# Order and timing of loads, 16-row broadcasts, a pool for unit 29 and a bank left out, in the last stage of an attention block with a gated MLP

## The chip, the cores and the metric

The kernel runs on one core of a Trainium2 chip. TensorE (PE) multiplies matrices into PSUM, VectorE (DVE), ScalarE (ACT) and GpSimd (POOL) work on tiles, and SyncE (SP) issues nearly all DMAs from one queue, in program order. The metric is the device time of one execution in microseconds (us). Before the change it is 1626.81 us, the median of three runs (1626.63 to 1628.37).

## The reference

```python
x = A_x                                   # (1, 2048, 512)
xn = layernorm(x)
s = attention(xn, A_wqkv) @ A_wo          # 32 heads of 16, softmax(q k^T / 4) v
h = relu(xn @ B_w1 + B_b1) ** 2           # 1792 wide
g = silu(h @ B_w2 + B_b2)
return x + s * g
```

Both branches read the normalised rows; the output joins them. All arithmetic is in float32: the kernel splits operands of projections into a high and a low part and multiplies them in three terms.

## The kernel before

Attention is cut into 32 units: a unit is four heads (a group, `qd = u // 4`) by 512 query columns (`qc = u % 4`). Units run one after the other. Each takes 16 slots, one for each block of 128 keys, so there are 512 slots, and slot `st` belongs to unit `st // 16`. In a slot PE computes scores for the exponentials (`exp_mm`, line 1260, exponential on ACT at line 1272), the scores again for row maxima of a unit further on (`max_mm`, line 320, maximum on DVE at line 327), the product of probabilities with v of two slots earlier (`pv_mm`, line 406, eight records a slot at the slot's end), and a share of the dense work that `dense()` hands out. PE, DVE, ACT, POOL and SP all keep the order in which the program was written.

The maxima of a unit end nine slots or so before it starts. `max_end` then puts the unit into `late` with a due time; when that comes, `shift` turns the maxima on DVE (lines 371 to 374), `keep` stores them to `sh_d` one slot later (line 380), and `back` reads them into the rows of `qe` (line 397, four small DMAs). Exponentials of a unit may start two slots after `back`. `later(n, fn)` runs `fn` at the start of the slot n slots on; everything due at one slot runs in the order in which it was put there, ahead of what the slot itself issues. A DMA whose wait isn't over holds all DMAs behind it on SP.

A unit's result leaves PSUM by `evac` (line 416) and is divided by its sums: these are stored to `r_d` (line 435), read back as a broadcast over 32 rows for each of four heads into the upper half of `hl` (line 440), and multiplied on POOL (line 446); POOL then splits the product (447, 448), and it is stored to `on_d` (455). Unit 29 goes another way: `unit_mid` copies it, and six slots later `unit_turn` transposes it on DVE (line 827) into the tiles `ttm0` and `ttm1`, so that sums can be divided there. Units 30 and 31 end in the same helper with other tiles.

Dense work: the MLP fills slots 4 to 451. Slots 452 and 453 have none. The output projection follows. `wo_part` (slots 454 to 485) computes 16 tiles of 128 rows by 512, k = 4c + tt, two slots a tile, with the first three quarters of the depth (three pieces `on_d[0..2]`, line 697, for column block c). `wo_load(c, ...)` brings the three pieces for a block: two into halves of a `ka` buffer, one into an `oc` buffer, 512 KB each; block 0's in two parts, at slot 452, and block c + 1 one piece a slot. `wo_ask(k)` asks for a tile's gate rows g (line 724) and its rows of x (`xr`, line 727, three buffers). When a tile is done, ACT copies it (line 774), POOL multiplies by g and adds xr (775, 776), and SP stores it to `sp_d` (778). `wo_last` (slots 486 to 510) adds the last quarter: PE, then a product on DVE that empties the bank (line 796), a sum (798), and the store of the output.

In `wo_part` four PSUM banks are shared by the projection tile and the row maxima. `bank()` takes the one that was taken longest ago, other than the current tile's. Tile 15 always takes `last_bank`.

Memory is handed out by pools on two stacks. `o3` holds the buffers `oc` and `xr` until slot 486; then `q6p` and `endp` open on the freed bytes.

These lines set the special slots:

```python
RUN = 454
PAIR = (484, 485)
MAXIMA = {465: 5, 481: 5, 484: 2, 485: 0}
TWO = (2, 3, 452, 453)
GAPS = (24,)
```

Of the kernel before, what the change touches and what calls it, by code (L numbers as in the profile page):

```python
# [9 lines left out]
F32 = mybir.dt.float32  # L10
F32R = mybir.dt.float32r
AF = mybir.ActivationFunctionType
ALU = mybir.AluOpType
# [4 lines left out]
P = 128  # L18
# [3 lines left out]
DH = 16  # L22
# [5 lines left out]
NU = NQ * 4  # L28
# [29 lines left out]
def kernel(  # L58
# [11 lines left out]
    nc = tc.nc  # L70
# [44 lines left out]
    with ExitStack() as ph:  # L115
# [81 lines left out]
        late = []  # L197
# [4 lines left out]
        def later(n, fn):  # L202
            if n:
                waiting.append((now[0] + n, fn))
            else:
                fn()
# [124 lines left out]
        def max_end(g):  # L331
            for u in [u for u, n in left.items() if n == 0]:
                del left[u]
                m4 = m4s[u % 2]
                nc.vector.tensor_reduce(m4[:, :16], mxs[u], axis=AX.X, op=ALU.max)
                mxs[u] = m4
                late.append((g + {0: 0, 3: 8, 29: 0, 30: 2, 31: 0}.get(u, 6), u))
            u, s = divmod(g, 16)
            if u >= NU:
                return  # L340
            qd, qc = divmod(u, 4)
            if qd == 0:
                if qc == 2 and s % 2 == 0 and s < 12:
                    load_k(1, s // 2)
                if qc == 3 and 9 <= s < 15:
                    load_k(1, s - 3)
            else:
                if qc == 2 and qd + 1 < NQ and s % 2 == 0:
                    load_k(qd + 1, s // 2)
                if qc == 3 and qd + 1 < NQ and s % 2 == 0 and s < 8:  # L350
                    load_k(qd + 1, 8 + s // 2)
            if u == 3 and s == 8:
                for j in range(2):
                    rows = slice(64 * j + 3 * DH, 64 * j + 4 * DH)
                    nc.sync.dma_start(
                        rot["ka"][3][rows, :].bitcast(F32), rot["ka"][2][rows, :].bitcast(F32)
                    )
            at = (12, 14) if u == 1 else (8, 9)
            if s in at:
                load_q_pair(u, "qe", at.index(s), qes.setdefault(u, []))  # L360
            at = (6, 10) if u == 1 else (7, 11)
            if s in at and u + 1 < NU:
                load_q_pair(u + 1, "qm", at.index(s), qms.setdefault(u + 1, []))
# [73 lines left out]
        def evac_back(u, ev):  # L437

            ev["hl"] = pools["n"].tile([P, 2, 512], F32R, name="hl")
            nc.sync.dma_start(  # L440
                ev["hl"][:, 1].bitcast(F32), r_d[u][:, None, :].to_broadcast([4, 32, 512])
            )

        def evac_norm(u, ev):
            ot, hl = ev["ot"], ev["hl"]
            nc.gpsimd.tensor_tensor(ot, ot, hl[:, 1].bitcast(F32), op=ALU.mult)  # L446
            nc.gpsimd.tensor_scalar(hl[:, 0], ot, 1.0, 0.0, op0=ALU.mult, op1=ALU.add)
            nc.gpsimd.tensor_tensor(hl[:, 1], ot, hl[:, 0].bitcast(F32), op=ALU.subtract)

# [184 lines left out]
        def right(stk, name, bufs):  # L634
            return stk.enter_context(tc.tile_pool(name=name, bufs=bufs, side="right"))
# [15 lines left out]
        def wo_pools():  # L651
            wos["f"] = right(wstk, "fp", 4)
            wos["oc1"] = right(wstk, "oc1p", 1)
            tp = tail["p"] = right(wstk, "tailp", 1)
            for tt in range(4):
                tail[3, tt] = tp.tile([P, D], F32, name=f"ts{tt}")
            left = ph.enter_context(tc.tile_pool(name="xpl", bufs=1))
            more = [left.tile([P, 512], F32, name=f"xl{i}") for i in range(3)]
            pool = right(wstk, "xpr", 1)
            more += [pool.tile([P, 512], F32, name=f"xr{i}") for i in range(NXR)]  # L660
            more += [vs["tiles"][0][:, 512 * i : 512 * i + 512] for i in range(2)]
            rot["pt"] = more + rot["pt"]
            wos["oc3"] = right(o3, "oc3p", 2)

        def wo_small():
# [53 lines left out]
        def wo_ask(k):  # L719

            c, tt = divmod(k % 16, 4)
            t0 = c * 512 + tt * P
            g = wos["f"].tile([P, D], F32, name="g", bufs=6)
            nc.sync.dma_start(g, g_d[t0 : t0 + P, :])
            if k < 16:
                t = wos["oc3"].tile([P, D], F32, name="xr", bufs=3)
                nc.sync.dma_start(t, xf[t0 : t0 + P, :])
            elif c < 3:
                t = wos["f"].tile([P, D], F32, name="s")
                nc.sync.dma_start(t, sp_d[t0 : t0 + P, :])  # L730
            else:
                t = tail[c, tt]
            wos[k] = g, t

        def bank():
            mine = wos["banks"]
            n = next(n for n, t in enumerate(mine) if t is not wos["tile"])
            mine.append(mine.pop(n))
            return mine[-1]

        def wo_part():
            wos["banks"] = [pm.tile([P, 512], F32, name="pm_t") for _ in range(3)]
            wos["banks"].append(pd.tile([P, 512], F32, name="pd_t"))
            last_bank = wos["banks"][2]
            wos["tile"] = None
            for c in range(4):
                for tt in range(4):
                    k = 4 * c + tt
                    if c < 3 and tt == (1 if c == 0 else 0):
                        wo_load(c + 1, [0, 1, 2])  # L750
                    if k < 14:
                        wo_ask(k + 2)
                    if k == 14:
                        wo_load(0, [3])
                        wo_ask(16)
                        wo_ask(17)
                    old = wos["tile"]
                    if k < 15:
                        ps = bank()
                        if old is not None:  # L760
                            wos["banks"].sort(key=lambda t: t is old)
                    else:
                        ps = last_bank
                        wos["banks"].sort(key=lambda t: t is last_bank)
                    wos["tile"] = ps
                    t0 = c * 512 + tt * P
                    g, xr = wos.pop(k)
                    if c == 3:
                        s = tail[c, tt]
                    else:  # L770
                        s = wos["f"].tile([P, D], F32, name="s")

                    def post():
                        nc.scalar.activation(s, ps, AF.Copy)
                        nc.gpsimd.tensor_tensor(s, s, g, op=ALU.mult)
                        nc.gpsimd.tensor_tensor(s, s, xr, op=ALU.add)
                        if c < 3:
                            later(2, lambda s=s, t0=t0: nc.sync.dma_start(sp_d[t0 : t0 + P, :], s))

                    yield from halves(wo_terms(ps, wos["t", c], tt, [0, 1, 2]), (9,), post, 1)  # L780
            wos["banks"] = None
# [29 lines left out]
        def load_q6(c):  # L811

            q = wos["q", c] = wos["q6"].tile([P, 2, 512], F32R, name=f"q6{c}")
            for h in range(2):
                nc.sync.dma_start(
                    q[64 * h : 64 * h + 64].bitcast(F32),
                    on_d[3][:, :64, c * 512 : (c + 1) * 512].rearrange("k p t -> p k t"),
                )
# [2 lines left out]

        def unit_turn(po, i, which=""):

            t = tail["e"].tile([P, 256], F32, name=f"tt{which}{i}")
            nc.vector.transpose(t, po[:, 256 * i : 256 * i + 256])
            sm = tail["e"].tile([P, 8], F32, name=f"tsm{which}{i}")
            return t.rearrange("p (b r) -> p b r", r=32), sm

        def unit_back(ot, rows, sm):
# [640 lines left out]
        def dense():  # L1472
            mp = ExitStack()
            yield from mlp_tasks(mp)
            mp.close()
            early.close()
            wo_pools()
            wo_load(0, [0, 1, 2])
            wo_ask(0)
            wo_ask(1)  # L1480
            for _ in range(2):
                yield [], None
            later(10, wo_small)
            yield from wo_part()
            for c in range(3):
                if c == 0:
                    o3.close()
                    wos["q6"] = right(wstk, "q6p", 1)
                    tail["e"] = right(wstk, "endp", 1)
                    later(10, lambda: load_q6(3))  # L1490
                yield from wo_last(c)

# [212 lines left out]
```

## Time and profile before

| | |
|---|---|
| median of three runs | 1626.81 us (1626.63 to 1628.37) |
| profiled execution | 1627.33 us |
| its span, first to last instruction | 1625.5 us |
| granted TensorE clock, mean | 0.999 |
| PE, DVE, ACT, POOL busy | 99%, 84%, 73%, 32% |
| DMA over the span | 209.45 MB, mean 129 GB/s |

How rows read: a timeline row has the start in us from the span's start, the duration, the engine, the line, the operation, what it writes and reads, and the count of merged instructions; in brackets stands idle time of the engine just before, and what ended it. SPq rows are DMA issues, not transfers. Matmuls overlap, so rows of PE overlap too. A windows row has, for a stretch, the busy time and count of PE, PE's weight loads, DVE, ACT and POOL, the granted clock, the mean busy share of the 16 DMA engines and the GB/s that they moved. A waits row has who waited for whom: us in total, times, the longest. A row of the groups has busy time, mean ns, and idle time before.

### The profile page before, as it was taken

Reading aid. Unit: us, or ns where it says so; the run is one execution under the profiler, and the core shown is the slowest. Engines: PE = TensorE matmul, PEld = TensorE weight load, DVE = VectorE, ACT = ScalarE, POOL = GpSimd, SP = SyncE. Lnnn points to the kernel's source line nnn. Section 1 sums busy time; section 2 is a strip of 40 time slices with the busy share of each in tenths; the row PEclk is TensorE's granted clock in tenths of the full one; section 3 lists DMA queues with packets and bytes.
Section 4 is the critical chain, followed back from the end, with each engine's and each line's share of the span. In section 5 each row is a group of like instructions: output and inputs, shape, how many; then the busy total and the mean of one; then the engine's idle time right before and its main releaser. Section 6 shows DMA issues by size and latency. Waiting matters only on the chain.

```text
span 1625.5 us, 36023 instructions
## 1 busy us (share of the span) xinstructions
PE 1609.1 (99%) x13660; PEld 936.6 (58%) x13660; DVE 1362.3 (84%) x2363; ACT 1189.8 (73%) x2350; POOL 521.9 (32%) x550
## 2 busy tenths in 40 slices
PE   8999999999999999999999999999999999999998
PEld 6899665556545654664466456645654565445543
DVE  6486888888888888888888888888888888887755
ACT  7212777777777777877777777777777777778876
POOL 6437667133113310321133112311331133214521
PEclk9999999999999999999999999999999999999999
DMA  8877556434333333434333334423442252237664
GB/s 301 232 237 233 173 163 157 127 95 130 79 104 97 101 93 85 128 87 110 83 114 96 87 87 126 116 66 84 131 122 62 73 157 72 61 109 225 186 197 168
DMA packets 164036, 209.45 MB, mean 129 GB/s; under 512 B 59000, under 2 KB 78968, under 8 KB 162296
## 3 DMA queue, kind: packets, MB, share of 16 engines
q1 hardware_dynamic: 163576, 206.63, 44.7%
q8 instruction: 108, 1.77, 0.5%
q14 instruction: 64, 0.52, 0.1%
q10 hardware_dynamic: 288, 0.52, 0.1%
HBM read 149.17 MB, written 56.34 MB: 126 GB/s over the span
## 4 chain that ended last, share of the span: by engine, by line
PE 97%; DVE 1%; DMA 1%; ACT 0%; issue 0%; SPq 0%; POOL 0%; ACTq 0%; POOLq 0%
PE po L406 31%; PE pd_t L258 19%; PE pm_t L320 17%; PE se L1260 14%; PE pd_t L226 5%; PE pm_t L1136 4%; PE pm_t L226 1%; PE pd_t L1136 1%; PE se L1106 1%; PE se L1040 1%; PE se L320 1%; DVE mx L327 1%; PE pm_t L1222 0%; DMA sh_d<-sh 0%; PE pd_t L1106 0%
## 5 line engine op out<-in xcount | busy, mean ns | idle before, releaser
L327 DVE TENSOR_REDUCE mx<-pm_t 128x1 f32<-128x512 f32 x1910 | 1187.8, 683 | 164.4 <-PE pm_t L320 70.4
L1272 ACT ACTIVATE pt<-se 128x512 f32<-128x512 f32 x1894 | 976.0, 612 | 236.5 <-PE se L1260 194.8
L320 PE MATMUL pm_t<-ka,qm 64*128 64x512 f32 x1910 | 761.3, 419 | 0.1
L1260 PE MATMUL se<-qe,ka 64*128 64x512 f32 x2005 | 677.9, 396 | 0.8 <-ACT pt L1272 0.5
L406 PE MATMUL po<-pt,v 128*32 128x512 f32 x3820 | 520.8, 605 | 0.1
L320 PEld LDWEIGHTS pm_t<-ka,qm 64*128 64x128 f32 x1910 | 335.2, 184 | 237.2 <-DVE mx L327 224.9
L1260 PEld LDWEIGHTS se<-qe,ka 64*128 64x128 f32 x2005 | 339.1, 184 | 20.6 <-ACT xr L1272 1.7
L258 PEld LDWEIGHTS pd_t<-xc,w1s 64*128 64x128 f32 x2352 | 292.1, 187 | 82.2 <-issue 82.2
L258 PE MATMUL pd_t<-xc,w1s 64*128 64x256 f32 x2352 | 332.3, 288 | 0.0
L258 PE MATMUL pd_t<-w2t,hT 64*128 64x512 f32 x1080 | 300.4, 410 | 0.0
L258 PEld LDWEIGHTS pd_t<-w2t,hT 64*128 64x128 f32 x1080 | 179.1, 184 | 82.4 <-issue 75.5
L562 POOL TENSOR_TENSOR r<-r 128x512 f32<-128x512 f32 x56 | 58.3, 1041 | 370.5 <-ACT r L559 370.5
L406 PEld LDWEIGHTS po<-pt,v 128*32 128x32 f32 x3820 | 76.7, 108 | 146.9 <-issue 125.6
L581 POOL TENSOR_TENSOR u<-u,b_t 128x512 f32<-128x512 f32 x16 | 20.6, 1286 | 319.2 <-ACT u L580 285.4
L327 DVE TENSOR_REDUCE mx<-se 128x1 f32<-128x512 f32 x121 | 77.9, 686 | 26.2 <-PE se L320 26.2
L446 POOL TENSOR_TENSOR ot<-ot,hl 128x512 f32<-128x512 f32 x29 | 37.2, 1283 | 173.9 <-DMA hl<-r_d 90.4
L559 ACT ACTIVATE r<-pd_t,b_t 128x256 f32<-128x256 f32 x112 | 47.0, 471 | 57.2 <-PE pd_t L258 55.0
L100 POOL TENSOR_TENSOR hT<-r,hT 128x512 fp32r<-128x512 f32 x56 | 72.3, 1291 | 4.7
L1136 PE MATMUL pm_t<-xT,wr_t 64*128 64x512 f32 x408 | 73.8, 388 | 0.0
L226 PE MATMUL pd_t<-w2t,hT 64*128 64x512 f32 x264 | 68.8, 393 | 0.0
L1136 PEld LDWEIGHTS pm_t<-xT,wr_t 64*128 64x128 f32 x408 | 59.4, 185 | 1.9
L1272 ACT ACTIVATE xr<-se 128x512 f32<-128x512 f32 x82 | 44.0, 607 | 9.1 <-PE se L1260 8.5
(171 smaller groups left out, 1352.1 us busy)
## 6 DMA issues: line engine op xcount, KB each, us to landing
w1s<-w_d SPq DMA_DIRECT2D x196, 256.0 KB
qm<-q_d SPq DMA_DIRECT2D x384, 32.0 KB
ka<-k_d SPq DMA_DIRECT2D x96, 128.0 KB
qe<-q_d SPq DMA_DIRECT2D x384, 32.0 KB
q_d<-hl SPq DMA_DIRECT2D x16, 512.0 KB
g<-g_d SPq DMA_DIRECT2D x32, 256.0 KB
k_d<-hl SPq DMA_DIRECT2D x15, 512.0 KB
hl<-r_d SPq DMA_DIRECT2D x29, 256.0 KB
```

Source lines behind the costliest of these rows:

```text
L100: (lo or nc.gpsimd).tensor_tensor(dst[1], raw, dst[0].bitcast(F32), op=ALU.subtract)
L226: mm = nc.tensor.matmul(out_, lh(r), rh(r), start=first_ and lane == 0, stop=last_ and lane == 1, skip_group_check=True,)
L258: mm = nc.tensor.matmul(out_, lh(r), rh(r), start=first_ and lane == 0, stop=last_ and lane == 1, skip_group_check=True,)
L320: nc.tensor.matmul(ps, qms[u][p][64 * j : 64 * j + 64, qb * P : (qb + 1) * P], kas[qd, p][64 * j : 64 * j + 64, kc * 512 : (kc + 1) * 512] ...
L327: return nc.vector.tensor_reduce(mxs[u][:, c, kc : kc + 1], ps, axis=AX.X, op=ALU.max)
L406: nc.tensor.matmul(po[32 * j : 32 * j + 32, :], vs[qd][:, (4 * kb + j) * VW : (4 * kb + j) * VW + 32], pts[j], start=(kb == 0), stop=(kb = ...
L446: nc.gpsimd.tensor_tensor(ot, ot, hl[:, 1].bitcast(F32), op=ALU.mult)
L559: nc.scalar.activation(r[:, i], ps[:, i * CW : (i + 1) * CW], AF.Relu, bias=b1_t[:, fo : fo + 1])
L562: nc.gpsimd.tensor_tensor(r, r, r, op=ALU.mult)
L1136: mm = nc.tensor.matmul(out_, lh(r), rh(r), start=first_ and lane == first, stop=last_ and lane != first, skip_group_check=True,)
L1260: nc.tensor.matmul(se, kas[qd, j // 2][b : b + 64, kb * P : (kb + 1) * P], qes[u][j // 2][b : b + 64, :], start=True, stop=True,)
L1272: return nc.scalar.activation(pts[j], se, AF.Exp, scale=0.25)
```

## The change

Six edits, all in the last stage (slots 452 to 487):

- Unit 29's `shift` is due two steps later, which is one slot later (slot 452 instead of 451); its `keep` and `back` follow.
- For units 27 to 31 `evac_back` reads the sums as four DMAs of 16 rows each into a tile `rb` of its own, instead of one DMA of 4 x 32 rows into `hl`. Units 27 and 28 alone come here. `rb` is filled with ones once, on POOL, when the pools open; `evac_norm` multiplies by it.
- Column block 3 is loaded from tile 10 on (slot 474) instead of tile 8 (slot 470).
- `wo_ask(k + 2)` runs one slot later, through `later(1, ...)`, for tiles 0 to 13.
- Tile 14 may not take `last_bank`.
- Unit 29's `unit_turn` takes its tiles from a pool `endm`, opened behind `endp`, and no longer from `endp`.

```diff
@@ max_end
-                late.append((g + {0: 0, 3: 8, 29: 0, 30: 2, 31: 0}.get(u, 6), u))
+                late.append((g + {0: 0, 3: 8, 29: 2, 30: 2, 31: 0}.get(u, 6), u))
@@ evac_back
-            nc.sync.dma_start(
-                ev["hl"][:, 1].bitcast(F32), r_d[u][:, None, :].to_broadcast([4, 32, 512])
-            )
+            if u < NU - 5:
+                nc.sync.dma_start(
+                    ev["hl"][:, 1].bitcast(F32), r_d[u][:, None, :].to_broadcast([4, 32, 512])
+                )
+                return
+            ev["rb"] = tail["rb"]
+            for j in range(4):
+                nc.sync.dma_start(
+                    ev["rb"][32 * j : 32 * j + DH],
+                    r_d[u][j : j + 1].to_broadcast([DH, 512]),
+                )
@@ evac_norm
-            nc.gpsimd.tensor_tensor(ot, ot, hl[:, 1].bitcast(F32), op=ALU.mult)
+            rb = ev["rb"] if "rb" in ev else hl[:, 1].bitcast(F32)
+            nc.gpsimd.tensor_tensor(ot, ot, rb, op=ALU.mult)
@@ wo_pools
+            tail["rb"] = right(o3, "rbp", 1).tile([P, 512], F32, name="rb")
+            nc.gpsimd.memset(tail["rb"], 1.0)
             wos["oc3"] = right(o3, "oc3p", 2)
@@ bank
-            n = next(n for n, t in enumerate(mine) if t is not wos["tile"])
+            n = next(n for n, t in enumerate(mine) if t is not wos["tile"] and t is not wos["kept"])
@@ wo_part
-            wos["tile"] = None
+            wos["tile"] = wos["kept"] = None
...
-                    if c < 3 and tt == (1 if c == 0 else 0):
+                    if c < 3 and tt == (1, 0, 2)[c]:
                         wo_load(c + 1, [0, 1, 2])
                     if k < 14:
-                        wo_ask(k + 2)
+                        later(1, lambda k=k: wo_ask(k + 2))
...
                     if k < 15:
+                        wos["kept"] = last_bank if k == 14 else None
                         ps = bank()
+                        wos["kept"] = None
@@ unit_turn
-        def unit_turn(po, i, which=""):
+        def unit_turn(po, i, which="e"):
 
-            t = tail["e"].tile([P, 256], F32, name=f"tt{which}{i}")
+            t = tail[which].tile([P, 256], F32, name=f"tt{which}{i}")
...
-            sm = tail["e"].tile([P, 8], F32, name=f"tsm{which}{i}")
+            sm = tail[which].tile([P, 8], F32, name=f"tsm{which}{i}")
@@ dense
                     tail["e"] = right(wstk, "endp", 1)
+                    tail["m"] = right(wstk, "endm", 1)
```

## The prediction

> **What bounds the kernel now.** I read the page's shares and chain first, then TensorE's (PE's) timeline from 1449 us on, where the diff acts, then the timelines of SP's DMA queue, VectorE (DVE), GpSimd (POOL) and ScalarE (ACT) around each hole in PE, then windows for the DMA engines.
>
> ```profile
> span 1625.5 us, 36023 instructions
> ...
> PE 1609.1 (99%) x13660; PEld 936.6 (58%) x13660; DVE 1362.3 (84%) x2363; ACT 1189.8 (73%) x2350; POOL 521.9 (32%) x550
> ...
> PE 97%; DVE 1%; DMA 1%; ACT 0%; issue 0%; SPq 0%; POOL 0%; ACTq 0%; POOLq 0%
> ```
>
> PE is busy 99% of the span and 97% of the chain that ended last, so the change can win only the holes that its stretch holds. Each slot ends with eight records of line 406, so the distance between two such groups is the length of a slot.
>
> ```profile
> 1452.81 1.06 PE L406 MATMUL po<-pt,v 128*32 128x512 f32 x8
> 1454.66 0.47 PE L226 MATMUL pm_t<-wot,ka 64*128 64x512 f32 x1 [0.79 <-DMA ka<-on_d]
> 1456.94 0.62 PE L406 MATMUL po<-xl,v 128*32 128x512 f32 x2
> ...
> 1460.23 1.06 PE L406 MATMUL po<-xr,v 128*32 128x512 f32 x8
> ...
> 1525.97 1.07 PE L406 MATMUL po<-xr,v 128*32 128x512 f32 x8
> ...
> 1527.77 0.47 PE L1260 MATMUL se<-qe,ka 64*128 64x512 f32 x1 [0.30 <-DMA qe<-sh_d]
> ...
> 1528.99 0.46 PE L1260 MATMUL se<-qe,ka 64*128 64x512 f32 x1 [0.49 <-ACT pt L1272]
> ...
> 1530.78 1.07 PE L406 MATMUL po<-xr,v 128*32 128x512 f32 x8
> ...
> 1534.06 0.62 PE L406 MATMUL po<-pt,v 128*32 128x512 f32 x1
> ```
>
> An undisturbed slot of this stage takes 3.28 us (1530.78 to 1534.06). Two slots are longer here: slot 454 took 4.13 us (1452.81 to 1456.94; its hole is labelled with the first loads of the output projection), slot 476 took 4.81 us (1525.97 to 1530.78; unit 30's shift rows arrive late, and the exponentials pile up behind them). They exceed a slot by 0.85 and 1.53 us. Two more follow.
>
> ```profile
> 1553.97 0.62 PE L406 MATMUL po<-xr,v 128*32 128x512 f32 x1
> ...
> 1555.50 0.50 PE L226 MATMUL pm_t<-wot,ka 64*128 64x512 f32 x1 [0.47 <-ACT ts L774]
> 1555.51 0.50 PE L1260 MATMUL se<-qe,ka 64*128 64x512 f32 x1
> 1555.84 0.39 PE L226 MATMUL pm_t<-wot,ka 64*128 64x512 f32 x1
> ...
> 1557.79 0.62 PE L406 MATMUL po<-xr,v 128*32 128x512 f32 x1
> ...
> 1567.02 0.50 PE L226 MATMUL pd_t<-wot,oc 64*128 64x512 f32 x1 [1.10 <-DVE g L796]
> ```
>
> Slot 484 (tile 15) took 3.82 us, 0.54 too long: it waits for ACT to empty tile 14's bank. Slot 488 has a hole of 1.10 us: tile 17 waits for VectorE to empty tile 16. Together the four holes are 4.0 us, 0.25% of the time. That is the most that the change can win, and 0.2% (3.25 us), about what a measurement of this kernel can tell from no change, lies just inside it.
>
> **Part by part.** The profiled execution took 1627.33 us for a span of 1625.5; the median shown is 1626.81, 0.52 lower. I subtract from the profiled time and quote the result against the median.
>
> *Unit 29's shift, a slot later.* The queue shows the hole's cause.
>
> ```profile
> 1448.76 0.42 SPq L153 DMA_DIRECT2D qm<-q_d  x1
> 1451.76 0.34 SPq L380 DMA_DIRECT2D sh_d<-sh  x1
> 1452.14 0.95 SPq L697 DMA_DIRECT2D ka<-on_d  x2
> 1453.19 0.41 SPq L697 DMA_DIRECT2D oc<-on_d  x1
> ```
>
> SP was free at 1449.2, but next in its order stood the store of unit 29's shift, which waited for DVE until 1451.76; the six loads of column block 0 stood behind it. In the new order they go first: the first load at about 1449.2 instead of 1452.14, ready by 1451.7 at the 2.5 us that it took before (1452.14 to 1454.66); PE wants it at 1453.87 (1452.81 + 1.06). The third piece leaves at about 1450.2, is ready by 1452.7 and wanted 1.5 us after the first. So the hole goes: -0.85. DVE's four shift operations now fall between two pairs of row maxima, the same work in the same stretch. The shift's store follows the six loads and four asks, and the four reads of it block SP until it lands; with one exponential a slot gained from slot 454 on, unit 29's (slot 464 by rights) start no earlier than slot 460, at about 1457 + 5 x 3.28 = 1473, and the reads should be in by 1462.5 (2.6 MB of loads and asks at the 302 GB/s below from 1449.2 on, 2.5 us to land, 2.1 us of reads), so this costs 0. If that cover were gone, the hole would look like slot 476's, 1.5 us.
>
> *Column block 3, two tiles later; asks one slot later.*
>
> ```profile
> 1511.08 0.19 DVE L374 SCALAR_TENSOR_TENSOR sh<-tr,sh 128x32 fp32r<-128x32 f32 x1
> ```
> ```profile
> 1515.04 0.38 SPq L697 DMA_DIRECT2D ka<-on_d  x1
> ...
> 1517.16 0.38 SPq L697 DMA_DIRECT2D ka<-on_d  x1
> 1517.64 1.07 SPq L380 DMA_DIRECT2D sh_d<-sh  x1
> ...
> 1519.52 0.56 SPq L697 DMA_DIRECT2D oc<-on_d  x1
> 1525.22 2.12 SPq L397 DMA_DIRECT2D qe<-sh_d  x4
> ```
> ```profile
> SPq L727 <- POOL s L776: 16.3, 4, 6.0
> ```
> ```profile
> 1515.00:1523.00 8.00, 8.00 (x68) 4.42 (x68) 6.40 (x11) 7.03 (x15) 3.93 (x4) 1.00 0.91 302
> ```
>
> Unit 30's shift is stored at 1517.64 behind two 512 KB pieces, and its reads can leave only at 1525.22, when the store has landed: 7.6 us. The DMA engines were 91% busy at 302 GB/s. Without the two pieces the store leaves two issues earlier (0.9 us) and finds 1.05 MB less ahead of it, 3.5 us at 302 GB/s: it lands near 1520.8, and the reads end near 1523 instead of 1527.3. PE needs 1.53 us of this, and 0.85 more because it now arrives earlier: 2.4 of 4.4 us. So -1.53 (between 0, if SP and not the data is late, and -1.53).
>
> What is late next is block 3 itself, wanted in slot 478. Behind the reads SP has to issue one store, two asks, four broadcasts, piece 1, a store, piece 2, two asks, piece 3: the last of twelve leaves 11 issues of about 0.47 us later, at 1528.2. The data of these is 3.3 MB, 10.9 us at 302 GB/s: ready near 1534 at worst. PE wants piece 1 at 1532.75 (1534.06 + 1.06 - 0.85 - 1.52) and piece 3 six of nine steps later, (3.28 - 1.06) x 6/9 = 1.5 us, at 1534.2. That is a thin cover, so I bound this by 0 and +2.0 and take 0, because SP should also be earlier: it had spent 16.3 us in four waits of an ask for POOL's add, and the new order puts stores and loads ahead of such asks. The asks are made two tiles ahead (13 us); one slot less costs 0, and uncovered it would hold POOL, not PE.
>
> *Broadcasts to 16 rows.* Two of the 29 units change (27 and 28): one DMA of 128 rows becomes four of 16, so three more issues each on SP (1.4 us, counted above) and half the bytes. A fill of 128x512 is new in slot 452, on POOL, which is busy 32% of the span; its twin below took 0.53 us: 0 on PE, 0.53 if it were uncovered.
>
> ```profile
> 1528.80 0.54 SPq L440 DMA_DIRECT2D hl<-r_d  x1
> ```
> ```profile
> 1536.55 1.28 POOL L446 TENSOR_TENSOR ot<-ot,hl 128x512 f32<-128x512 f32 x1 [6.50 <-DMA hl<-r_d]
> ```
> ```profile
> L672 POOL MEMSET ts<- 128x512 f32 x1 | 0.5, 527 | 0.0
> ```
> ```profile
> 1504.60 3.67 SPq L681 DMA_DIRECT2D ts<-in_A_wo_dram  x8
> ```
> ```profile
> 1505.00:1508.00 3.00, 3.00 (x26) 1.59 (x24) 2.40 (x5) 2.80 (x7) 1.13 (x2) 1.00 0.29 67
> ...
> 1538.00:1540.00 2.00, 2.00 (x18) 1.39 (x16) 1.20 (x3) 1.23 (x4) 1.92 (x3) 1.00 0.27 104
> ```
>
> The old broadcast took 7.75 us from issue to POOL's start, and at 1538 to 1540, when the rest had drained, a share of 0.27 was still moving: about 4 of 16 engines worked off a backlog. Sixteen-row loads ran alone from 1505 to 1508 at 67 GB/s, more than three times the 21 GB/s that one engine made at 302 GB/s over 0.91 x 16. So they spread, and the backlog should vanish. PE does not wait for POOL here: 0, between 0 and the +2.0 above.
>
> Eight 16-row loads left SP within 3.67 us, 0.46 each, so four are 1.8 us of SP's time if their landings overlap. The Trainium skill's page "DMA: Bandwidth & Descriptors" (section Rules for kernel authors) speaks against the edit: transfers under 64 KB pay mostly overhead and should be joined into one. Were the 2.5 us from issue to use of the first load paid four times in series, block 3 would wait 10 us instead of 1.8, and the sum would turn into a loss of some 5 us; that is rival (3). The same section has a rule for it: an outermost dimension below 16 keeps a DMA on at most that many engines. By that the old broadcast, whose outer dimension is 4, sits on four engines, with which the trace's 0.27 agrees, and each new one may use sixteen, which no run shows yet.
>
> *A bank left out.* Tile 14 took the bank that tile 15 must have. Now it takes the next one, whose last maximum was emptied in time for a maximum at the same moment of the old slot 482. But the first maximum of slot 484 then falls on tile 14's bank.
>
> ```profile
> 1554.81 0.64 ACT L774 ACTIVATE ts<-pm_t 128x512 f32<-128x512 f32 x1
> ```
>
> ACT's copy ends at 1555.45. Tile 15 could start at 1555.03 (1553.97 + 1.06), that maximum one step of 0.33 later (1555.51 to 1555.84) at 1555.36; it waits some 0.14 us instead of 0.47 earlier. -0.40 (between 0 and -0.54).
>
> *Own memory for unit 29's turn.*
>
> ```profile
> 1564.30 1.29 POOL L776 TENSOR_TENSOR ts<-ts,xr 128x512 f32<-128x512 f32 x1
> ```
> ```profile
> 1565.62 0.77 DVE L827 STREAM_TRANSPOSE ttm<-ot 128x256 f32<-128x256 f32 x2 [2.39 <-ACT xr L1272]
> ```
>
> DVE's transpose starts 0.03 us after POOL's last add, which shares no operand with it, and DVE's emptying of tile 16 stands behind it. What they share is memory: the pool opens on bytes freed by the pool of the asked x rows. The new pool is opened at the same place and lies in the same freed bytes (4,096 for q6, 8,256 for the rest, 2,112 for this one, of 16,384 freed). If a new pool waits for the whole of the one it replaces, as this row suggests, nothing changes. 0, between 0 and -1.10.
>
> Sum: -0.85 - 1.53 - 0.40 = -2.78. From the profiled 1627.33 this gives 1624.55, against the median 1624.0.
>
> **Rivals.** (1) The transpose no longer waits for the add, because the waits go by tile: slot 488's hole goes as well, 1622.9. For it: the transposed tiles' own bytes lie in a load buffer long free, not in the x rows'. Against it: so they did before, and it waited. (2) The late rows stay late, because SP is the late one, or block 3's third piece now stalls slot 478: 1.5 us come back, 1625.5. For it: SP stores the shift only 6.4 us after DVE had it (1511.27). Against it: 7.6 us for a 32 KB store is data ahead of it. (3) Slower: the four broadcasts crowd one engine, or run in series, ahead of piece 1. At the old pace (7.75 us for 32 rows on each of four) 64 rows take 15.5 us; sent by about 1526, piece 1 is then there at 1541.5 instead of 1532.75, 8.75 us lost against 2.78 won: 1632.8. It decides once the delay passes 6 us. Against it: 67 GB/s above, and eight such loads at 0.46 us each. (4) The change does nothing that PE sees: the DMA engines or SP keep the same end, 1626.8. Against it: the wait of 1449.2 to 1451.76 is plain order.
>
> **How the numbers follow.** Forecast 0.60, rivals (1) 0.14, (2) 0.16, (3) 0.06, (4) 0.04. The likeliest gives 1624.0, itself within 1623.3 to 1624.8 (the bank's bounds and the runs' scatter). From 1622.5 to 1626.1 leaves out (3), (4) and a little of (1) and (2), about 0.15. Below 1623.56 lie most of (1) (0.12) and a quarter of the forecast (0.15), since half a microsecond of scatter carries it there: faster 0.27; above 1630.06 (3): slower 0.06; the rest, 0.67, within 0.2%.
>
> **What would show it.** Slot 454 and slot 476 at 3.28 us with no hole in PE; the store of unit 30's shift followed by its reads within 5 us; POOL's first product of unit 28 without a wait; no share near 0.27 after the broadcast; slot 484 at 3.4 us; the hole of 1.10 us before tile 17 still there, with the transpose again right behind POOL's add. I am wrong if slot 478 shows a hole labelled oc or ka, if the hole at tile 17 goes, or if a hole appears where unit 29's exponentials start.

## The result, and the profile after

The changed kernel takes 1625.06 us (median of 22 runs, 1624.01 to 1626.6), the kernel before took 1627.96 us beside it (22 runs, 1625.95 to 1629.86). The ratio is 0.9984, 95% interval 0.9977 to 0.9990: 2.9 us less, where 2.78 was forecast. Here the kernel before is a median of 22 runs; the 1626.81 us ahead of the prediction was a median of three. The profiled execution took 1625.59 us for a span of 1623.7. From the page after, the span, PE's shares and the chain:

```profile
span 1623.7 us, 36039 instructions
...
PE 1609.1 (99%) x13660; PEld 937.1 (58%) x13660; DVE 1363.5 (84%) x2363; ACT 1189.8 (73%) x2350; POOL 522.1 (32%) x551
...
PE 98%; DVE 1%; ACT 0%; issue 0%; DMA 0%; POOL 0%; POOLq 0%; ACTq 0%
```

PE is busy for the same 1609.1 us as before; only its idle time shrank. PE's timeline after, with the products that end a slot, and the one hole that is left of the four:

```profile
1448.51 1.06 PE L406 MATMUL po<-pt,v 128*32 128x512 f32 x8
...
1453.98 1.06 PE L406 MATMUL po<-pt,v 128*32 128x512 f32 x8
1457.27 0.62 PE L406 MATMUL po<-xl,v 128*32 128x512 f32 x2
...
1526.26 1.07 PE L406 MATMUL po<-xr,v 128*32 128x512 f32 x8
...
1529.54 1.07 PE L406 MATMUL po<-xr,v 128*32 128x512 f32 x8
...
1532.82 0.62 PE L406 MATMUL po<-pt,v 128*32 128x512 f32 x1
...
1552.72 0.62 PE L406 MATMUL po<-xr,v 128*32 128x512 f32 x1
...
1556.08 0.62 PE L406 MATMUL po<-xr,v 128*32 128x512 f32 x1
...
1559.49 1.06 PE L406 MATMUL po<-xr,v 128*32 128x512 f32 x8
...
1565.44 0.49 PE L226 MATMUL pd_t<-wot,oc 64*128 64x512 f32 x1 [1.09 <-DVE g L809]
...
1610.44 1.90 PE L406 MATMUL po<-xr,v 128*32 128x512 f32 x16
```

And three rows of the kernel before that the next sums need:

```profile
1447.34 1.06 PE L406 MATMUL po<-pt,v 128*32 128x512 f32 x8
...
1561.07 1.06 PE L406 MATMUL po<-xr,v 128*32 128x512 f32 x8
...
1612.03 1.90 PE L406 MATMUL po<-xr,v 128*32 128x512 f32 x16
```

Slot 454 went from 4.13 to 3.29 us (1453.98 to 1457.27), slot 476 from 4.81 to 3.28 (1526.26 to 1529.54), and slot 484 from 3.82 to 3.36 (1552.72 to 1556.08). Slot 485 went from 3.28 to 3.41 (1556.08 to 1559.49), and the hole at tile 17 stayed. The stretch from the first to the last of these rows was 164.69 us long and is 161.93: 2.76 us less. I use this stretch below for all kernels, because ahead of it executions differ by themselves (last section).

The SP queue after, around the two orders that changed:

```profile
1450.38 0.93 SPq L708 DMA_DIRECT2D ka<-on_d  x2
...
1452.89 0.47 SPq L708 DMA_DIRECT2D oc<-on_d  x1
...
1458.56 0.38 SPq L380 DMA_DIRECT2D sh_d<-sh  x1
...
1514.31 0.40 SPq L380 DMA_DIRECT2D sh_d<-sh  x1
...
1518.51 2.10 SPq L397 DMA_DIRECT2D qe<-sh_d  x4
...
1522.11 1.82 SPq L447 DMA_DIRECT2D rb<-r_d  x4
...
1526.75 0.60 SPq L708 DMA_DIRECT2D oc<-on_d  x1
```

Block 0's six loads stand ahead of unit 29's shift (1458.56). Unit 30's shift is read back 4.2 us after its store (7.6 before). Counted from the first PE row of the stretch, its reads leave at 70.00 us (1518.51 - 1448.51); before it was 77.88. The four broadcasts went out within 1.82 us, and block 3's last piece left at 1526.75.

### The profile page after: what moved, and what is told of

The parts are those of the page before. It is cut to its first block, busy times and chain, and to the rows that moved or that the text cites. A ratio compares the mean times of both kernels' runs of the same rounds, so it can differ in the third digit from the quotient of the medians.

```text
span 1623.7 us, 36039 instructions
## 1 busy us (share of the span) xinstructions
PE 1609.1 (99%) x13660; PEld 937.1 (58%) x13660; DVE 1363.5 (84%) x2363; ACT 1189.8 (73%) x2350; POOL 522.1 (32%) x551
## 4 chain that ended last, share of the span: by engine, by line
PE 98%; DVE 1%; ACT 0%; issue 0%; DMA 0%; POOL 0%; POOLq 0%; ACTq 0%
PE po L406 31%; PE pd_t L258 20%; PE pm_t L320 17%; PE se L1273 14%; PE pd_t L226 5%; PE pm_t L1149 4%; PE pd_t L1149 1%; PE pm_t L226 1%; PE se L1119 1%; PE se L1053 1%; PE se L320 1%; DVE mx L327 1%; PE pm_t L1235 0%; PE pd_t L1119 0%; PE po L1053 0%
## 5 line engine op out<-in xcount | busy, mean ns | idle before, releaser
L258 PEld LDWEIGHTS pd_t<-w2t,hT 64*128 64x128 f32 x1080 | 179.5, 185 | 83.2 <-issue 75.4
L226 PEld LDWEIGHTS pd_t<-w2t,hT 64*128 64x128 f32 x264 | 47.1, 185 | 6.1 <-issue 0.3
```

Source lines behind the costliest of these rows:

```text
L226: mm = nc.tensor.matmul(out_, lh(r), rh(r), start=first_ and lane == 0, stop=last_ and lane == 1, skip_group_check=True,)
L258: mm = nc.tensor.matmul(out_, lh(r), rh(r), start=first_ and lane == 0, stop=last_ and lane == 1, skip_group_check=True,)
```

## The experiments

All of them in one table. The stretch is that of the last section. "Reads" is the time from the stretch's start to the first read of unit 30's shift. Slots are in us, and 3.28 is undisturbed (1.89 for slot 488); they are taken from unrounded starts, so the last digit can differ by 0.01 from the rows shown. The stretch, the reads and the slots are of one profiled execution of each kernel. Where no count of runs is given, the time is of that one execution too.

How far can single executions be trusted? Four kernels have the same loads, asks and broadcasts up to slot 478: the change, the one without the bank, and the two that move the turn's memory. Their reads left at 70.00 to 70.80 us, so differences of the reads below 0.8 us mean little. Their slots up to 478 agree within 0.04 us.

The diffs of the three runs called "alone" are against the kernel before, all others against the changed kernel.

| kernel | stretch, against before | reads | 454 | 476 | 478 | 484 | 488 |
|---|---|---|---|---|---|---|---|
| before | 164.69 | 77.88 | 4.13 | 4.80 | 3.28 | 3.83 | 3.06 |
| after | -2.76 | 70.00 | 3.29 | 3.28 | 3.28 | 3.35 | 3.06 |
| shift alone | +1.61 | 77.95 | 3.29 | 6.29 | 3.28 | 3.83 | 3.06 |
| block 3 alone | +0.88 | 72.04 | 4.13 | 3.28 | 5.77 | 3.82 | 3.07 |
| asks alone | -1.55 | 76.55 | 4.14 | 3.31 | 3.28 | 3.83 | 3.05 |
| after, asks back | -1.17 | 72.19 | 3.29 | 3.29 | 4.88 | 3.36 | 3.07 |
| after, block 3 back | -2.76 | 75.02 | 3.28 | 3.28 | 3.28 | 3.36 | 3.06 |
| after, block 3 a tile later still | +3.25 | 70.99 | 3.29 | 3.29 | 7.12 | 3.36 | 3.06 |
| after, old broadcasts | -1.72 | 72.02 | 3.29 | 3.29 | 4.25 | 3.35 | 3.07 |
| after, four broadcasts of 32 rows | -2.69 | 70.59 | 3.29 | 3.29 | 3.30 | 3.35 | 3.06 |
| after, bank not left out | -2.25 | 70.80 | 3.29 | 3.28 | 3.28 | 3.83 | 3.06 |
| after, turn in the old pool | -2.69 | 70.63 | 3.29 | 3.29 | 3.31 | 3.35 | 3.06 |
| after, turn's pool opened early | -3.73 | 70.49 | 3.28 | 3.29 | 3.29 | 3.36 | 1.89 |
| shift, asks, bank, early pool | -3.03 | 76.36 | 3.28 | 3.98 | 3.29 | 3.35 | 1.89 |

**The shift alone.**

```diff
-                late.append((g + {0: 0, 3: 8, 29: 0, 30: 2, 31: 0}.get(u, 6), u))
+                late.append((g + {0: 0, 3: 8, 29: 2, 30: 2, 31: 0}.get(u, 6), u))
```

> The kernel before with one edit: unit 29's shift falls due two slots later. The theory (the store of that shift stood ahead of column block 0's six loads in SP's order): slot 454 takes 3.28 us instead of 4.13, and slots 476 (4.80), 484 (3.83) and 488 (3.06) stay: 0.85 us less. The rival (the DMA engines or the data are late, or the hole moves on to where unit 29's rows are wanted): slot 454 keeps 4.1, or a slot from 455 to 465 grows by 0.5 us or more.

It took 1630.15 us, beside 1628.24 before. Slot 454 came down as expected, but slot 476 grew to 6.29 and slot 477 to 3.87. The hole did not go: it moved on, and became dearer. PE's timeline in slot 476, and windows whose seventh number is the granted clock:

```profile
1529.08 0.46 PE L1260 MATMUL se<-qe,ka 64*128 64x512 f32 x1 [0.87 <-DMA qe<-sh_d]
...
1530.24 0.47 PE L1260 MATMUL se<-qe,ka 64*128 64x512 f32 x1 [0.43 <-ACT pt L1272]
```
```profile
1530.70:1532.00 1.30, 1.30 (x10) 1.25 (x8) 0.86 (x2) 1.19 (x2) 0.06 (x1) 0.54 1.04 328
1532.00:1533.00 1.00, 1.00 (x5) 0.33 (x2) 0.84 (x2) 0.60 (x1) 0.00 (x0) 0.50 0.93 274
1533.00:1534.60 1.60, 1.60 (x11) 0.23 (x10) 0.37 (x1) 0.60 (x1) 0.00 (x0) 0.62 0.97 245
```

PE is 0.85 us early, while the reads leave as late as before (77.95 against 77.88), so PE waits longer. Then the granted clock falls to 0.50 for 3.4 us (1530.8 to 1534.2, inside the windows shown). At 0.54, 0.50 and 0.62 those windows hold 2.2 us of full-speed work in 3.9 us, so 1.7 us went to the clock alone; it is about half of the 3.6 by which the two slots exceed 3.28, and as much as the whole loss of 1.61 in the stretch. Slot 471 lost 0.32 as well; DVE waited 0.37 us in it for a DMA of another unit's sums.

**Block 3 alone.**

```diff
-                    if c < 3 and tt == (1 if c == 0 else 0):
+                    if c < 3 and tt == (1, 0, 2)[c]:
```

> The kernel before with one edit: the loads of column block 3 two tiles later. The theory (two 512 KB pieces stood ahead of unit 30's shift): the store of that shift and its four reads lie within 5 us instead of 7.6, slot 476 takes 3.28 us instead of 4.80, but with the broadcast of 128 rows still whole the last piece of block 3 comes late as it does in the change with the old broadcast, so slot 478 takes about 4.2 instead of 3.28: some 0.6 us less in all. A rival (SP itself is late): slot 476 stays over 4.5. Another (the broadcast does not matter once the asks keep their old place): slot 478 stays at 3.28.

It took 1628.26 us beside 1628.24. Slot 476 is cured, and more is lost in slot 478. PE's timeline there, and the window around it:

```profile
1536.03 0.49 PE L226 MATMUL pm_t<-wot,ka 64*128 64x512 f32 x1 [1.56 <-DMA ka<-on_d]
...
1537.37 0.49 PE L226 MATMUL pm_t<-wot,oc 64*128 64x512 f32 x1 [0.38 <-DMA oc<-on_d]
```
```profile
1536.00:1538.00 2.00, 1.59 (x12) 0.98 (x12) 1.29 (x2) 0.66 (x2) 1.40 (x2) 1.00 0.32 114
```

Block 3's pieces come too late, by 1.5 us more than I expected. Idle time of 1.94 us did not lower the clock here.

**The asks alone.**

```diff
                     if k < 14:
-                        wo_ask(k + 2)
+                        later(1, lambda k=k: wo_ask(k + 2))
```

> The kernel before with one edit: the asks for y and x rows one slot later. The theory (an ask costs nothing where it stands, only data and the order of the shift count): slots 454, 476, 484 and 488 all stay within 0.1 us of 4.13, 4.80, 3.83 and 3.06. The rival (asks wait for GpSimd's adds and hold SP's queue; 16.3 us of such waits): slot 476 falls by 0.5 us or more by itself.

The theory fell. Slot 476 went from 4.80 to 3.31 us by the asks alone, with block 3's pieces still ahead of the shift, and the kernel took 1625.42 us. The SP queue of the kernel before shows where SP lost its time:

```profile
1479.06 0.52 SPq L724 DMA_DIRECT2D g<-g_d  x1
1484.05 0.33 SPq L727 DMA_DIRECT2D xr<-in_A_x_dram  x1
1484.43 1.83 SPq L455 DMA_DIRECT2D on_d<-hl  x4
...
1487.33 3.73 SPq L153 DMA_DIRECT2D qm<-q_d  x6
```

And that with the asks a slot later:

```profile
1480.47 1.73 SPq L455 DMA_DIRECT2D on_d<-hl  x4
1483.76 0.34 SPq L778 DMA_DIRECT2D sp_d<-s  x1
...
1485.65 3.64 SPq L153 DMA_DIRECT2D qm<-q_d  x6
...
1516.87 0.55 SPq L380 DMA_DIRECT2D sh_d<-sh  x1
...
1523.62 2.13 SPq L397 DMA_DIRECT2D qe<-sh_d  x4
```

In both, SP stands until about 1484 because of the same add on POOL, for 4.4 us before and for 1.5 us with the asks later. Before, four stores of a unit's result stood behind that wait. With the asks later, the wait stands at the store of `s`, and those four stores went out while SP would have waited. From there on SP is 1.7 us ahead (1485.65 against 1487.33), and it is still 1.6 us ahead at the reads (1523.62 against 1525.22; 1.33 counted from the stretch's start).

**The whole change with the asks back, and with block 3 back.**

```diff
-                        later(1, lambda k=k: wo_ask(k + 2))
+                        wo_ask(k + 2)
```

> The changed kernel with the asks back in their old place, a slot earlier; block 3 stays two tiles later, the broadcasts have 16 rows. Theory A (the whole broadcast was what made block 3 late when it was moved alone, 5.77 us in slot 478): slots 476 and 478 both take 3.28 us and the time is that of the change. Theory B (the asks that then stand ahead of block 3's pieces make them late): slot 478 takes 4 to 6 us, 1 to 2.5 us lost.

```diff
-                    if c < 3 and tt == (1, 0, 2)[c]:
+                    if c < 3 and tt == (1, 0, 0)[c]:
```

> The changed kernel with column block 3's loads back in their old place, two tiles earlier; asks, shift, broadcasts and bank stay changed. With the asks alone moved, slot 476 took 3.31 us: unit 30's rows were just in time, at a PE that still had the hole of slot 454. Theory (both are needed): with PE 0.85 us earlier they are late again, slot 476 takes 4.0 to 5.5 us, and 0.8 to 2 us are lost against the change. The rival (the asks alone do it, the move of block 3 is idle): slot 476 stays at 3.3 and the time is that of the change.

With the asks back it took 1626.26 us; slot 478 lost 1.6 us, so theory B held. PE's timeline of that kernel:

```profile
1534.61 0.49 PE L226 MATMUL pm_t<-wot,ka 64*128 64x512 f32 x1 [0.68 <-DMA ka<-on_d]
...
1535.96 0.50 PE L226 MATMUL pm_t<-wot,oc 64*128 64x512 f32 x1 [0.39 <-DMA oc<-on_d]
```

With block 3 back in its old place it took 1624.69 us and has the same stretch as the change, 161.93. Here the rival held: with the asks and the broadcasts changed, the move of block 3 brings nothing. The "reads" column shows why I was wrong to expect a loss. The reads left 1.5 us sooner than with the asks alone (75.02 against 76.55); the last experiment, with the old broadcasts and 76.36, puts most of that, 1.34 us, down to the split broadcasts.

**Block 3 a tile later still.**

```diff
-                    if c < 3 and tt == (1, 0, 2)[c]:
+                    if c < 3 and tt == (1, 0, 3)[c]:
```

> The changed kernel with column block 3 one tile later still, three in place of two. Theory (block 3's cover is thin, its last piece comes less than 1 us ahead of PE): the pieces leave about 6.5 us later, and slot 478 gets a hole of 2 to 6 us labelled with ka or oc. The rival (the cover is the 7 us that lie between the last piece's issue and PE's wish for it): slot 478 takes under 3.8 us.

It took 1630.82 us. Slot 478 took 7.12 and slot 479 5.43 us. The hole is the one expected, and again the clock fell:

```profile
1537.70 0.79 PE L226 MATMUL pm_t<-wot,oc 64*128 64x512 f32 x1 [1.72 <-DMA oc<-on_d]
```
```profile
1537.70:1540.00 2.30, 2.30 (x10) 1.03 (x14) 0.69 (x1) 1.18 (x2) 0.00 (x0) 0.50 0.77 261
1540.00:1543.80 3.80, 3.80 (x20) 2.14 (x14) 1.21 (x2) 1.26 (x4) 0.00 (x0) 0.50 0.51 142
```

Half speed over these 6.1 us is 3.05 of the 6.0 us lost in the two slots. So the cover in the changed kernel is thin, and there was no room for another tile.

**The broadcasts: the old ones, and four of 32 rows.**

```diff
-            if u < NU - 5:
+            if u < NU:
```

> The changed kernel with the one broadcast of 4 x 32 rows for units 27 and 28 instead of four of 16. Theory (the new broadcasts win nothing on PE, and the old one loads few DMA engines): POOL's first product of unit 28 waits some 5 to 7 us again, a DMA share near 0.25 shows after the broadcast has been asked for and the rest has drained, and block 3's pieces, asked for right behind it, land up to 4 us later; with some 7 us of cover slot 478 stays within 0.5 us of 3.28. Rival (the broadcast was needed for the gain): slot 478 longer by 1 to 4 us, with a hole labelled ka or oc.

```diff
-                    ev["rb"][32 * j : 32 * j + DH],
-                    r_d[u][j : j + 1].to_broadcast([DH, 512]),
+                    ev["rb"][32 * j : 32 * j + 32],
+                    r_d[u][j : j + 1].to_broadcast([32, 512]),
```

> The changed kernel with four broadcasts of 32 rows each, so the bytes of the old one in four DMAs. Theory (the old one was slow because it sat on four engines, not because of its bytes): POOL's first product of unit 28 starts with no wait, no share near 0.25 is left behind, PE as in the changed kernel. Rival (the bytes, or reading one row many times, made it slow): POOL waits several us as with the old one, and block 3's pieces land late.

With the old broadcasts it took 1626.55 us: slot 478 lost 0.97, where I had expected at most 0.5, so the theory fell; the rival had said 1 to 4. Of that kernel the issue of block 3's last piece, PE where it waited for it, and POOL's product of unit 27:

```profile
1527.47 0.65 SPq L708 DMA_DIRECT2D oc<-on_d  x1
```
```profile
1536.01 0.50 PE L226 MATMUL pm_t<-wot,oc 64*128 64x512 f32 x1 [0.70 <-DMA oc<-on_d]
```
```profile
1479.23 1.29 POOL L455 TENSOR_TENSOR ot<-ot,hl 128x512 f32<-128x512 f32 x1 [1.74 <-DMA hl<-r_d]
```

PE waited 0.70 us for the last piece, and POOL 1.74 us for unit 27's broadcast. In the changed kernel both waits are gone. The last piece was not late in leaving: it left 79.19 us into the stretch (1527.47 - 1448.28), and in the kernel without the bank at 79.05, where slot 478 still took 3.28. So its transfer took longer. Two other marks that I expected did not come: POOL's product of unit 28 did not wait at all, and no window of 2 us from 1530 to 1542 showed a DMA share under 0.57. With four DMAs of 32 rows, the same bytes as the old one DMA, the kernel took 1625.90 us and slot 478 3.30: the split does it, not the smaller size. By the Trainium skill, page "DMA: Bandwidth & Descriptors", section "Rules for kernel authors", an outermost dimension below 16 keeps a DMA on at most that many engines; the runs agree with that rule. Here this outweighed the advice of the Trainium skill, in the same section, to join transfers under 64 KB: four of 32 KB, issued within 1.82 us, beat one of 256 KB. No run joins the rows into one DMA with a longer outer dimension. With 32 rows the last piece of block 3 left 0.8 us later than in the change, counted from the stretch's start, and slot 478 just began to stall (3.30). The 32 rows are not the reason: in the kernel with the turn in the old pool, which has the broadcasts of the change, it left 0.8 us later too, and slot 478 took 3.31. So the cover is about that thick.

**The bank.**

```diff
-                        wos["kept"] = last_bank if k == 14 else None
+                        wos["kept"] = None
```

> The changed kernel without the bank that is left out for tile 14. The theory: slot 484 goes back from 3.35 to 3.83 us and slot 485 from 3.41 to 3.28: 0.35 us more, and no other slot moves. The rival (the earlier work ahead of it removes the wait by itself): slot 484 stays at 3.35.

It took 1625.79 us. Slot 484 went back to 3.83 and slot 485 to 3.28: 0.35 us, as expected. The stretch lost 0.51; most of the rest is in slot 492, which took 2.09 us instead of 1.92; why is open. PE's timeline shows the hole of before again:

```profile
1553.99 0.50 PE L226 MATMUL pm_t<-wot,ka 64*128 64x512 f32 x1 [0.47 <-ACT ts L787]
```

**The turn's memory: in the old pool, and in a pool opened early.**

```diff
-                    tail["m"] = right(wstk, "endm", 1)
+                    tail["m"] = tail["e"]
```

> The changed kernel with unit 29's turn back in the pool endp. Theory: that edit does nothing, so the hole before tile 17 stays at 1.1 us and slot 488 at 3.06 us, both as with it. Rival (own memory helped a little, or moved another wait): slot 488 longer by over 0.1 us, or a hole elsewhere.

```diff
             tail["rb"] = right(o3, "rbp", 1).tile([P, 512], F32, name="rb")
             nc.gpsimd.memset(tail["rb"], 1.0)
+            tail["m"] = right(wstk, "endm", 1)
             wos["oc3"] = right(o3, "oc3p", 2)
...
-                    tail["m"] = right(wstk, "endm", 1)
```

> The changed kernel with one difference: the pool of unit 29's turn is opened in slot 452, ahead of the load buffers, so it lies on no byte that the x rows use. Theory (the transpose waits for the whole pool whose freed bytes it takes): the transposes start right after slot 486's first DVE work, some 2.4 us earlier against POOL's add, the hole of 1.10 us before tile 17 goes, slot 488 takes 1.9 us instead of 3.06, and the time is 1.1 us below the changed kernel's (2.6 us below the kernel before becomes about 3.7, ratio 0.9977). Rival (the transpose waits for POOL itself, or DVE would be late for tile 16 anyway): hole and time as in the changed kernel, ratio 0.9984.

The changed kernel's DVE and POOL around tile 17:

```profile
1564.04 0.77 DVE L840 STREAM_TRANSPOSE ttm<-ot 128x256 f32<-128x256 f32 x2 [2.38 <-ACT xr L1285]
1564.73 0.65 DVE L809 TENSOR_TENSOR g<-pd_t,g 128x512 f32<-128x512 f32 x1
```
```profile
1562.71 1.29 POOL L789 TENSOR_TENSOR ts<-ts,xr 128x512 f32<-128x512 f32 x1
```

The transpose starts 0.04 us after POOL's add ends, as it did before. Putting the tiles into the old pool again changes nothing (1624.76 us, slot 488 3.06). Opening the pool on other bytes, ahead of the x rows' pool, does:

```profile
1561.24 0.76 DVE L841 STREAM_TRANSPOSE ttm<-ot 128x256 f32<-128x256 f32 x2
1563.11 0.69 DVE L810 TENSOR_TENSOR g<-pd_t,g 128x512 f32<-128x512 f32 x1 [1.11 <-POOL ts L789]
```

The transpose is now done before that add, tile 16's bank is empty by 1563.8, and slot 488 takes 1.89 us. This kernel took 1624.14 us (10 runs) against 1627.89, a ratio of 0.9978 (0.9969 to 0.9988); by the stretch, the shortest of this study, it beats the change by 0.97 us.

**Only what seemed to be needed.** The shift, the asks, the bank and the early pool, with block 3 and the broadcasts as in the kernel before:

```diff
-                    if c < 3 and tt == (1, 0, 2)[c]:
+                    if c < 3 and tt == (1, 0, 0)[c]:
...
-            if u < NU - 5:
+            if u < NU:
...
-            tail["rb"] = right(o3, "rbp", 1).tile([P, 512], F32, name="rb")
-            nc.gpsimd.memset(tail["rb"], 1.0)
+            tail["m"] = right(wstk, "endm", 1)
...
-                    tail["m"] = right(wstk, "endm", 1)
```

> The kernel before with four edits alone: unit 29's shift two slots later, the asks one slot later, the bank left out for tile 14, and the memory of unit 29's turn opened earlier, on other freed bytes. Column block 3 is loaded in its old place and the broadcasts are the old ones of 128 rows. Theory (these four carry all of the gain, block 3's move and the split broadcasts cancel each other): slots 454, 476 and 478 take 3.28 us, slot 484 3.35, slot 488 1.89, and the time is 3.9 us under the kernel before, a ratio of 0.9976. The rival (block 3's move or the split broadcasts add to the gain): slot 476 or 478 takes 3.8 us or more, and the ratio is 0.998 or above.

It took 1624.62 us (11 runs) against 1628.39, 0.9977 (0.9968 to 0.9986). The ratio is the theory's, and of the rival's two marks one was met: slot 476 took 3.98. POOL's product of unit 27 waited for its broadcast here too:

```profile
1478.49 1.29 POOL L455 TENSOR_TENSOR ot<-ot,hl 128x512 f32<-128x512 f32 x1 [1.65 <-DMA hl<-r_d]
```

The stores of that unit's result wait for POOL and hold SP, so the reads left at 76.36 us instead of the 75.02 of the kernel with block 3 back, and slot 476 lost 0.70. (That kernel also differs by the early pool, beside which the reads of the change left no sooner: 70.49 and 70.00.) So, by the slots of single executions, the split broadcasts are worth 0.7 us with block 3 in its old place and 1.0 with it moved. They do not merely cancel its move. The medians cannot show a difference of 0.7: this kernel and the one with the early pool are 3.77 and 3.75 us under the kernels before beside them, and their intervals overlap.

## Why the prediction was right, and where it was not

The forecast was of 2.78 us less, and 2.9 were measured. Quoted as a time it was 1624.0 us, likeliest between 1623.3 and 1624.8, and the median of 1625.06 lies above that. The edits are not the reason: the time was quoted against the three-run median of 1626.81, and over 22 runs the kernel before took 1627.96.

*Unit 29's shift: right in place and size, for the whole change.* Predicted -0.85, measured -0.84. The run alone adds what the prediction named only inside another step: the gain is kept only if unit 30's rows come 0.85 us earlier too. On its own the edit made the kernel slower in the one execution, by about what the clock took. No slot from 455 to 475 grew by more than 0.04 us in the changed kernel, so the hole feared where unit 29's exponentials start did not come.

*Column block 3 and the asks: right in size, wrong in cause.* Predicted -1.53, measured -1.52. The step failed where it gave all of this to the move of block 3 ("data ahead of" the store) and "0" to the asks. The asks alone won 1.49 of it; with the asks and broadcasts changed, the move won 0.00. The data ahead of the store are real: with the asks as before, moving block 3 brought the reads from 77.88 to 72.04 us. But PE needed little of this, and SP could give that by itself: the later asks alone brought them to 76.55. What counts is how long before slot 476 starts the reads leave. They left 0.19 us before it in the shift's run, 0.75 in the kernel before, 1.50 in the last experiment, 2.07 with the asks alone and 2.72 with block 3 back, and the slot took 6.29, 4.80, 3.98, 3.31 and 3.28 us. A little over 2 us is enough; the change has 7.75. The row that told it was quoted, 16.3 us of SP's waits for POOL; I used it as a reason for block 3's cover and did not ask which DMAs stood behind those waits. The bound that I wrote, "between 0, if SP and not the data is late", named the case and not its other remedy.

*Block 3's cover: right.* It was called thin, bounded by 0 and +2.0 and taken at 0. It is about 0.8 us in the changed kernel. One count in the working was off: the list from the store to piece 3 has thirteen issues and not twelve, so at 0.47 us each the last would leave at 1528.6 and not 1528.2; the bounds do not hang on it. Without the later asks 1.6 is lost, without the split broadcasts 1.0, and by block 3's move alone 2.5. So rival (2)'s second half, a stall in slot 478, was close, and the two edits that I costed at nothing are what keeps it away.

*Broadcasts: 0 in my sum, 0.7 to 1.0 by the runs.* The reading that four engines worked off a backlog fits, since four DMAs with the same bytes take the delay away; no view here shows the DMA engines one by one. Its price was wrong, because I counted only POOL's wait for unit 28, which PE does not feel. What PE feels is SP, which waits for POOL to finish unit 27, and block 3's pieces, which land later behind the one broadcast. The first of these is large only with the late shift: unit 27's product waited 1.65 to 2.41 us for its old broadcast in the three kernels with both, and 0 to 0.66 in the three with the old shift. Rival (3), the loss to a crowd of small DMAs, was wrong.

*The bank: right mechanism, 0.35 in place of 0.40.* The estimate for slot 484 fits better than its term: 3.35 measured, 3.4 named. The missing 0.13 us is in slot 485, which grew from 3.28 to 3.41. I had not followed the changed order of the banks into the next slot; what waits there I have not separated.

*Own memory: right.* 0, and the hole of 1.10 stayed. The reason held too: memory of its own does nothing while it lies in the freed bytes of the x rows' pool, and on other bytes the whole hole goes.

The sum came out at -2.76 in the stretch, against -2.78. That it came out so close is partly luck: two wrong zeros and one wrong owner did not show in it, since the edits depend on each other: +1.61, +0.88 and -1.55 alone for shift, block 3 and asks.

## What to carry to other kernels

A queue that issues in order has a price at each wait, and that price is what stands behind it: before crediting a gain to less data, ask whether moving a wait behind the work that it holds would do the same. When several edits touch one queue, cost them in each other's presence, since a gain at one hole moves the wish of the next. A pool that opens on freed bytes inherits the waits of the pool that freed them; open it on bytes that have long been idle.

## What I had not expected of the hardware

Short holes can halve the granted clock, and not reliably. Idle times of 0.87 and 0.43 us in the shift's run were followed by 3.4 us at 0.50 (1530.8 to 1534.2); 0.90 and 1.72 us in the run with block 3 later still by 6.8 us at 0.50 (1537.2 to 1544.0); 1.56 and 0.38 us in the run of block 3 alone by a clock of 1.00. Each is a single execution. The Trainium skill, page "TensorE: Matmul & The Clock Gate", section "HAM oscillation — how this bites in real kernels", puts the danger at gaps over about 3.4 us. These runs measured a drop after gaps half as long and less, so the measurement decides: the clock added 1.7 us to 1.30 us of idle time, and 3.05 to 2.62, so a small hole may cost more than twice its length. What sets it off is open. The drops lasted 3.4 us and twice 3.4 us; that would fit a clock set in steps of this length, where it matters how a hole falls on the steps, but no run tests it.

One operation far ahead of the change also varies by itself. It is the last step of a shift on DVE in slot 43. The first row is of the kernel before; the other two are of the changed kernel, with POOL's operation beside it:

```profile
286.46 0.19 DVE L374 SCALAR_TENSOR_TENSOR sh<-tr,sh 128x32 fp32r<-128x32 f32 x1
```
```profile
286.28 1.25 DVE L374 SCALAR_TENSOR_TENSOR sh<-tr,sh 128x32 fp32r<-128x32 f32 x1
```
```profile
286.19 1.30 POOL L457 TENSOR_TENSOR hl<-ot,hl 128x512 fp32r<-128x512 f32 x1
```

Slot 43 took 2.87 us with the one and 3.83 with the other. Among the other kernels, whose code there is the same, it took from 2.87 to 3.82. That is noise of nearly 1 us, and the reason why single executions are compared by the stretch. The traces point to POOL: the 1.25 us end 0.04 us after POOL's operation (287.53 against 287.49). In twelve of the fourteen kernels this step or the one before it (line 373) took longer than the 0.18 to 0.19 us of the others, up to 1.25, and in all twelve it ended 0.03 to 0.05 us after the POOL operation that was running. How long that is depends on when POOL's work falls, which shifts from execution to execution. No run moves either operation.
